# Delta rule and SoLU layer on one core: six batches of two chunks, off-diagonal Gram blocks copied by ScalarE from PSUM, first blocks of T read back by quarter

## Chip, cores and metric

The kernel runs on one core of one Trainium2 chip. The metric is device time in microseconds (us) for one execution. The median of three runs is 513.54 us (513.34 to 514.23). The core's engines run side by side, each in the order of its own program: PE (matmul), DVE, ACT, POOL, and SP, which here issues every DMA.

## What is computed

Two parts in a row. The first is a delta rule over 768 steps for 4 batches of 8 heads with 48 dimensions each; its output, seen as 3072 tokens of 384 numbers, goes through a layer with 1024 hidden units.

```python
k_n = k / (norm(k) + 1e-6)
for t in range(S):                       # S = 768
    y[t] = q[t] @ state
    v_old = k_n[t] @ state
    state = state + beta[t] * outer(k_n[t], v[t] - v_old)
x = y.transpose(0, 2, 1, 3).reshape(3072, 384)
h = x @ w_in                             # 384 x 1024
solu = h * softmax(h)
ln = (solu - mean) / sqrt(var + 1e-6) * g_ln
out = ln @ w_out                         # 1024 x 384
```

## The kernel before

**Tiling.** The 768 steps are cut into 12 chunks of C = 64. Within a chunk the recurrence is solved at once: with the Gram matrix of the chunk's keys a unit triangular 64x64 system has to be inverted for each (batch, head). The inverse is called T. Two batches with 8 heads each share the 128 partitions; such a pair is `bp`. A *unit* is one chunk of one pair, so there are 24 units, numbered here 0 to 23 (unit = 2 x chunk + pair). Each unit holds 128 tokens for the second part.

**Batches of inversions.** Inversion works on 32x32 diagonal blocks, one block for each partition ("lane"), for several units together. Such a group is a batch `m`; `chunks_of(m)` says which chunks it takes. Before, there are seven: chunk 0; chunks 1 and 2; 3 and 4; 5 and 6; 7 and 8; 9 and 10; chunk 11. So batches 0 and 6 have two units, the others four. For each batch:

- `load_kq`, `gram`: for each unit PE forms k k^T (`gram`) and k q^T (`qk`) in PSUM, ACT copies the first to `g`, DVE masks the second to `pm`, and SP stores `g` in DRAM as `gd`.
- `to_inv`: SP loads the diagonal blocks from `gd` into `ginv`, one block for each lane.
- `norms`: 19 small DVE operations on the diagonal (the first writes `rst`) give the norms of k, and two DVE products of 128x1024 prepare `ginv` and `y`. POOL then masks `y` (`affine_select`): this is the start of the inversion proper.
- `inv_step`: 30 steps, each a product `itmp` and a sum into `y`. In batches 0 and 1 DVE and POOL share them; in the others POOL does all.
- `inv_end`: ACT writes a transposed copy into `ginv`, SP stores `y` as `zd` and that copy as `xd`, and loads them back lane by lane: `zt` (diagonal blocks of T) and `gx`, `gy` (the off-diagonal Gram blocks from `gd`, the first diagonal blocks from `xd`).
- `tlevel`/`block_level`: for each unit two rounds of small matmuls (`mps<-zt,gx`, then `mps<-msb,gx` and `mps<-msb,gy`) give the off-diagonal block of T, which ACT copies into `zt`. They are called T1 and T2 below.

`chain(m, u)` then runs the recurrence for a unit: K·S (`kps`), the difference `r` on DVE, U = T r (`ups`), its state update (`cps`, into `st`) and the output `yps`, which is split into a high and a low half `xh`, `xl` and transposed by DMA (`xth`, `xtl`). `moe_h` forms h with 18 matmuls, its row maximum on DVE (the first `TENSOR_REDUCE st<-h` of a unit, used as its mark), exponent, product, sums and `pth`, `ptl`; `moe_out` has 24 matmuls `ops` with w_out, the correction by `csum` and the store `out_dram<-oc`.

**Order.** Nothing here is issued in the order in which it is written. A recorder collects all operations; `Recorder.order` is a list scheduler with its own costs, which picks for each engine the ready operation with the smallest priority, and `emit` (line 265) writes the result out. So every row of the profile has line L265, and tiles tell the operations apart. The priorities are numbers on a scale of units: chain of unit i at i, its h at i + 1.15, its output at i + 2.5. A batch whose first unit is f has its Gram products, its start (`begin`) and its T at fixed distances ahead of f; chain has an extra shift of -CH. On the chip each engine keeps the emitted order, and an instruction that waits holds up all that stand behind it on its engine. For SP this means that a DMA that waits for its data or its buffer holds up every later DMA.

Buffers come from small pools: `p10` is a ring of ten for the tags `kq` (kq tiles and the raw w_out), `ps_f` two PSUM buffers for `gram`, `qk` and `mps`, `ps_ch` two for the chain. Loads of w_in and w_out are converted by DVE, POOL and ACT (`wf`, `wg`, `wc_i`, `wc_o`) into two halves each; `column_sums` (`csum`) needs all of w_out.

Of the kernel before, what the change touches and what calls it, by code (L numbers as in the profile page):

```python
# [16 lines left out]
P = 128  # L17
C = 64
NC = S // C
NB = 7  # L20
CH = 1
SC = 64.0
SC2 = SC * SC
# [275 lines left out]


def chunks_of(m):
    return [ch for ch in (2 * m - 1, 2 * m) if 0 <= ch < NC]


@with_exitstack
def kernel(
# [223 lines left out]
    last0 = [None]  # L530

    def to_inv(m):
        gi = p2.tile([P, 32, 32], F32, tag="ginv", name=f"ginv_{m}")
        ginv[m] = gi
        for b in range(4):
            blk = b % 2
            for z in range(1 if len(units(m)) == 4 else 2):
                src = gdt[m].rearrange("t u h j -> t (u h) j")
                n = H * len(units(m))
                ls = slice(0, n)  # L540
                sp.dma_start(
                    kb=128, out=gi[32 * b + 16 * z : 32 * b + 16 * z + n],
                    in_=src[32 * b : 32 * b + 32, ls, blk * 32 : blk * 32 + 32].rearrange("j l i -> l j i"),
                )
# [32 lines left out]
    def inv_end(m):  # L577
        y, x1 = yt[m], ginv[m]
        act.copy(ns=1950, out=x1, in_=y.rearrange("p j i -> p i j"))
        zd = dr.tile([P, 32, 32], F32, tag="zd", name=f"zd_{m}")  # L580
        sp.dma_start(kb=512, out=zd, in_=y)
        xd = dr.tile([P, 32, 32], F32, tag="xd", name=f"xd_{m}")
        for r0 in (0, 64):
            sp.dma_start(kb=128, out=xd[r0 : r0 + 32], in_=x1[r0 : r0 + 32])
        zz = zt[m % 2]

        xx = p2.tile([P, 4 * H, 32], F32, tag="gx", name=f"gx_{m}")
        xy = p1.tile([P, 4 * H, 32], F32, tag="gy", name=f"gy_{m}")
        n = 16 * len(chunks_of(m))
        src = gdt[m].rearrange("t u h j -> t (u h) j")  # L590
        for b in range(4):
            blk = b % 2
            r0 = 32 * b
            rows = slice(r0, r0 + 32)
            sp.dma_start(kb=128, out=zz[rows, 0:n, blk * 32 : blk * 32 + 32], in_=zd[r0 : r0 + n].rearrange("l j i -> j l i"))
# [217 lines left out]
    for bp in range(2):
        add(once(-14 + .1 * bp, lambda bp=bp: load_kq(0, bp), lambda bp=bp: squares(bp)))
        add(gram(0, bp, -13.5 + .01 * bp))
        add(once(-9, lambda bp=bp: load_kv(0, bp), lambda bp=bp: fill_v(0, bp)))
        add(tlevel(0, bp, -12.9 + 0.1 * bp, -12.85 + 0.1 * bp))
# [12 lines left out]
    for m in range(1, NB):
        f = 4 * m - 2
        nu = len(units(m))
        e = f if m > 1 else f - 2.5
        for u in range(nu):
            tg = e - 9 + 0.9 * u if m > 1 else -11.2 + 0.05 * u
            ch, bp = units(m)[u]
            add(once(tg - 0.9 if m > 1 else -11.8, lambda ch=ch, bp=bp: load_kq(ch, bp)))
            add(gram(m, u, tg))  # L840
            t = e - 1.9 + 0.9 * u
# [5 lines left out]
        add(inversion(m, tn + 0.6, e - 2.6 if m > 1 else -10))  # L847
# [35 lines left out]
def _lay(q, k, v, beta, moe_w_in, moe_w_out, moe_g_ln):  # L883
# [45 lines left out]
```

## Time and profile before

| | |
|---|---|
| median of 3 runs | 513.54 us |
| profiled execution | 512.04 us |
| its span (first to last instruction) | 510.2 us |
| busy: PE, DVE, ACT, POOL | 368.2, 318.6, 192.9, 294.0 us |
| DMA | 180640 packets, 72.21 MB, queue 1 70.8% |
| granted TensorE clock, mean | 0.92 |

A row of the timeline gives the start (us from the span's start), the duration, the engine, the line, the operation, the tile written and those read, and the shapes; `xN` joins N equal ones in a row. In brackets stands how long the engine had been idle, and what ended that. SPq is SP's queue: there a row is the issue of a DMA, not its flight. In the groups of instructions the columns are busy time, mean duration in ns, and idle time before with its releaser. In the list of DMAs they are the count, the size of each and the median us from issue to landing.

### The profile page before, as it was taken

Reading aid. Unit: us, or ns where it says so; the run is one execution under the profiler, and the core shown is the slowest. Engines: PE = TensorE matmul, PEld = TensorE weight load, DVE = VectorE, ACT = ScalarE, POOL = GpSimd, SP = SyncE. Lnnn points to the kernel's source line nnn. Section 1 sums busy time; section 2 is a strip of 40 time slices with the busy share of each in tenths; the row PEclk is TensorE's granted clock in tenths of the full one; section 3 lists DMA queues with packets and bytes.
Section 4 is the critical chain, followed back from the end, with each engine's and each line's share of the span. In section 5 each row is a group of like instructions: output and inputs, shape, how many; then the busy total and the mean of one; then the engine's idle time right before and its main releaser. Section 6 shows DMA issues by size and latency. Waiting matters only on the chain.

```text
span 510.2 us, 18246 instructions
## 1 busy us (share of the span) xinstructions
PE 368.2 (72%) x7744; PEld 233.9 (46%) x7744; DVE 318.6 (62%) x791; ACT 192.9 (38%) x382; POOL 294.0 (58%) x506
## 2 busy tenths in 40 slices
PE   3510070689579488997598997787969797899974
PEld 3410070455346345665366564444635464566532
DVE  3599999887884383655088664256597355455670
ACT  2210241465522143536144544224345345454450
POOL 3378385966558998984016886008989898100000
PEclk9999999877876699998799998898989899999998
DMA  8685662987989949977999587985656866744332
GB/s 212 159 255 98 155 169 65 161 171 174 172 162 165 179 113 160 168 135 161 189 165 144 145 162 151 160 162 95 107 118 144 145 114 128 131 64 99 73 68 61
DMA packets 180640, 72.21 MB, mean 142 GB/s; under 512 B 165520, under 2 KB 168976, under 8 KB 180560
## 3 DMA queue, kind: packets, MB, share of 16 engines
q1 hardware_dynamic: 180560, 71.06, 70.8%
q8 instruction: 60, 0.98, 0.9%
q14 instruction: 20, 0.16, 0.1%
HBM read 37.21 MB, written 16.52 MB: 105 GB/s over the span
## 4 chain that ended last, share of the span: by engine, by line
POOL 28%; PE 22%; DVE 19%; issue 10%; DMA 9%; SPq 7%; ACT 4%; POOLq 0%; DVEq 0%; ACTq 0%
POOL y L265 13%; POOL itmp L265 11%; PE h L265 7%; SPq L265 7%; PE ops L265 7%; DVE y L265 5%; DVE itmp L265 4%; DMA zt<-zd 3%; DMA ginv<-gd 3%; PE mps L265 2%; DVE wf L265 2%; DVE rst L265 1%; DVE st L265 1%; PE kps L265 1%; PE yps L265 1%
## 5 line engine op out<-in xcount | busy, mean ns | idle before, releaser
L265 POOL TENSOR_TENSOR y<-y,itmp 128x84 f32<-128x84 f32 (+16 forms) x190 | 100.7, 530 | 14.6
L265 POOL TENSOR_TENSOR itmp<-y,ginv 128x84 f32<-128x84 f32 (+16 forms) x190 | 93.3, 491 | 14.0
L265 DVE TENSOR_REDUCE st<-h 128x1 f32<-128x1024 f32 x24 | 29.3, 1222 | 87.5 <-PE h L265 82.2
L265 PE MATMUL qk<-kq 48*64 48x64 f32 x768 | 40.4, 269 | 24.9 <-DVE pm L265 15.6
L265 PE MATMUL gram<-kq 48*64 48x64 f32 x768 | 43.2, 270 | 18.8 <-DMA kq<-kq_dram 11.5
L265 POOL TENSOR_TENSOR st<-st,nhalf 128x1 f32<-128x1 f32 x24 | 13.2, 551 | 64.1 <-DVE st L265 64.1
L265 PEld LDWEIGHTS gram<-kq 48*64 48x64 f32 x768 | 37.5, 178 | 25.7 <-ACT g L265 6.3
L265 PEld LDWEIGHTS <-pth 128*128 128x128 f16 x384 | 37.6, 99 | 25.5 <-issue 1.7
L265 PE MATMUL h<-win_hi,xtl 128*128 128x512 f16 x144 | 45.4, 419 | 5.3 <-DVE pr L265 2.6
L265 PE MATMUL mps<-zt,gx 32*32 32x32 f32 x768 | 13.5, 205 | 48.6 <-issue 28.9
L265 PE MATMUL h<-win_lo,xth 128*128 128x512 f16 x144 | 46.7, 421 | 1.7 <-POOL win_lo L265 1.7
L265 PEld LDWEIGHTS qk<-kq 48*64 48x64 f32 x768 | 35.8, 178 | 25.3 <-DVE pm L265 16.1
L265 PEld LDWEIGHTS <-xth 128*128 128x128 f16 x288 | 28.4, 105 | 39.7 <-issue 14.8
L265 PE MATMUL ops<-wout_hi,ptl 128*128 128x384 f16 x192 | 38.7, 345 | 8.7 <-DMA ptl<-pl 6.8
L265 PE MATMUL h<-win_hi,xth 128*128 128x512 f16 x144 | 43.4, 411 | 0.0
L265 ACT ACTIVATE e<-h,st 128x1024 f32<-128x1024 f32 x24 | 26.7, 1114 | 38.0 <-DVE st L265 26.4
L265 POOL TENSOR_SCALAR_AFFINE_SELECT y<-y 128x1024 f32<-128x1024 f32 x7 | 9.4, 1346 | 53.5 <-DVE y L265 53.5
L265 DVE TENSOR_SCALAR st<-st 128x1 f32<-128x1 f32 (+1 forms) x216 | 35.5, 165 | 5.6
L265 PE MATMUL ops<-wout_lo,pth 128*128 128x384 f16 x192 | 36.9, 334 | 0.0
L265 PEld LDWEIGHTS mps<-zt,gx 32*32 32x32 f32 x768 | 10.1, 117 | 56.9 <-issue 34.8
L265 PE MATMUL ops<-wout_hi,pth 128*128 128x384 f16 x192 | 35.5, 326 | 0.0
L265 PE MATMUL cps<-u,kv 64*64 64x48 f32 x704 | 28.9, 235 | 9.1 <-ACT u L265 3.2
(94 smaller groups left out, 860.4 us busy)
## 6 DMA issues: line engine op xcount, KB each, us to landing
kq<-kq_dram SPq DMA_DIRECT2D x48, 192.0 KB, 4.5
kv<-kv_dram SPq DMA_DIRECT2D x24, 384.0 KB, 4.3
gd<-g SPq DMA_DIRECT2D x48, 128.0 KB, 3.3
out_dram<-oc SPq DMA_DIRECT2D x24, 192.0 KB, 2.2
zd<-y SPq DMA_DIRECT2D x7, 512.0 KB, 2.6
wi<-w_in_dram SPq DMA_DIRECT2D x6, 512.0 KB, 4.4
wo<-w_out_dram SPq DMA_DIRECT2D x8, 384.0 KB, 4.0
ginv<-gd SPq DMA_DIRECT2D x20, 128.0 KB, 4.2
```

The source lines that it names most:

```text
L265: fn(*[real(a) for a in args], **{k: real(a) for k, a in kw.items()})
```

## The change

There are six batches of two whole chunks, four units each. Batch 0 now has four units (kn is loaded and squared for four; beta no longer has doubled entries). The off-diagonal Gram blocks no longer go through DRAM: ACT copies them from PSUM right after `g`, two copies of 32x256 for each unit, into `gx`. The first diagonal blocks of T were loaded twice, into `gx` and `gy`; now a tile `xx` takes each block once, in the partition quarter in which T2 reads it, with 16 DMAs of 16 KB for each batch. For batches 0 and 1 `zt` and `xx` are loaded in two halves, of two units each. The Gram products of batch 0 use the PSUM buffers of the chain, and two of its `g` copies the tile `e`. The raw w_in tiles share the ring `kq`, and their loads get an earlier priority. The priorities of `begin`, of batch 0's T and chain and of batch 2's Gram products are new numbers.

```diff
-NB = 7
+NB = NC // 2
 def chunks_of(m):
-    return [ch for ch in (2 * m - 1, 2 * m) if 0 <= ch < NC]
+    return [2 * m, 2 * m + 1]
...
     def load_w_in(k, q, t0, t1):
-        raw = p3.tile([P, 512], w_in.dtype, tag="pr", name=f"wi_{k}_{q}")
+        raw = (p3 if k < 2 and q < 1 or k < 1 else p10).tile([P, 512], w_in.dtype, tag="pr" if k < 2 and q < 1 or k < 1 else "kq", name=f"wi_{k}_{q}")
...
     def gram(m, u, t0):
         act.copy(out=g, in_=gps_)
+        if u == 0:
+            gxt[m] = p3.tile([P, 4 * H, 32], F32, tag="gx", name=f"gx_{m}")
+        for b2 in range(2):
+            act.copy(out=gxt[m][C * b2 + 32 : C * b2 + 64, H * u : H * u + H], in_=gps_[C * (1 - b2) + 32 : C * (1 - b2) + 64, :, 0:32])
...
     def inv_end(m):
-        xx = p2.tile([P, 4 * H, 32], F32, tag="gx", name=f"gx_{m}")
-        xy = p1.tile([P, 4 * H, 32], F32, tag="gy", name=f"gy_{m}")
...
-            if blk == 0:
-                for t, r1 in ((xx, r0), (xy, r0 + 32)):
-                    sp.dma_start(kb=128, out=t[r1 : r1 + 32, 0:n], in_=xd[r0 : r0 + n].rearrange("l j i -> j l i"))
-            else:
-                sp.dma_start(kb=128, out=xx[rows, 0:n], in_=src[rows, 0:n, 0:32])
+        xx = p2.tile([P, 4, 4, 32], F32, tag="xx", name=f"xx_{m}")
+        for us_ in ((0, 2), (2, 4)) if m < 2 else ((0, 4),):
+            n = us_[1] - us_[0]
+            l = slice(H * us_[0], H * us_[1])
+            for r0 in (0, 64):
+                lanes = slice(r0 + l.start, r0 + l.stop)
+                src = xd[lanes].rearrange("(u x h) j i -> j x u h i", u=n, x=2)
+                for u in range(n):
+                    for x in range(2):
+                        r1 = r0 + 32 * x
+                        sp.dma_start(kb=16, out=xx[r1 : r1 + 32, us_[0] + u], in_=src[:, x, u])
+                for blk in range(2):
...
+                    sp.dma_start(kb=32 * n, out=zz[rows, l, blk * 32 : blk * 32 + 32], in_=zd[lanes].rearrange("l j i -> j l i"))
...
-        f = 4 * m - 2
-        e = f if m > 1 else f - 2.5
+        f = 4 * m
...
-        tn = e - 5.4 if m > 1 else -10.8
+        tn = f - 5.4 if m > 2 else f - 7 if m > 1 else -10.8
...
-        add(chain(m, u, i, i + 0.13, i + 0.25), -CH)
+        add(chain(m, u, i, i + 0.13, i + 0.25), -CH if m else -14)
```

How this moves instructions is shown at three places. A name carries its batch, or its chunk and pair, and then a running number.

The first is DVE around its share of batch 1's inversion. Before, `itmp_1_30` is the last step of that inversion; then follow `wf` and `pm`, and only then the state `st_0` of the first chunk and its `xl_0_0`.

```order
L265 TENSOR_TENSOR itmp_1_30_0_1036<-y_1_657,ginv_1_553 128x10
L265 TENSOR_TENSOR y_1_657<-y_1_657,itmp_1_30_0_1036 128x10
L265 TENSOR_SCALAR wf_1_1_1041<-wi_1_1_479 128x512
L265 SCALAR_TENSOR_TENSOR wf_1_1_1041<-wi_1_1_479,wf_1_1_1041 128x512 x2
L265 TENSOR_TENSOR pm_3_0_1050<-qk_3_0_910,mask_93 128x512
L265 COPY st_0_1055<-cps_0_0_854 128x384
L265 SCALAR_TENSOR_TENSOR xl_0_0_1070<-yps_0_0_856,xh_0_0_921 128x384
```

After, the product that opens the inversion of batch 1 (`y_1`), then the state and `xl_1_0` of the second chunk, then the inversion's first step:

```order
L265 TENSOR_TENSOR y_1_1106<-ginv_1_874,nb_1_1072 128x1024
L265 TENSOR_SCALAR wg_0_1171<-wo_0_1079 128x384
L265 SCALAR_TENSOR_TENSOR wg_0_1171<-wo_0_1079,wg_0_1171 128x384
L265 TENSOR_TENSOR st_0_936<-st_0_936,cps_1_0_1134 128x384
L265 SCALAR_TENSOR_TENSOR xl_1_0_1202<-yps_1_0_949,xh_1_0_1193 128x384
L265 TENSOR_TENSOR itmp_1_1_0_1215<-y_1_1106,ginv_1_874 128x30
L265 TENSOR_TENSOR y_1_1106<-y_1_1106,itmp_1_1_0_1215 128x30
```

What moved: the chain of chunks 0 and 1 for pair 0 stood behind the whole inversion of batch 1 and now stands ahead of its first step.

The second is SP where the Gram blocks of batch 2 are loaded for the inversion (`ginv_2`), in the order after. `pth_0_1` and `ptl_0_1` belong to unit 1, `g_5_1` is the last Gram product of batch 2, and `xth_2_0` belongs to the chain of unit 4:

```order
L265 DMA kq_5_1_1952<-kq_dram 48x1024 x2
L265 DMA_TRANSPOSE pth_0_1_2000<-ph_0_1_1955 128x8x128
L265 DMA_TRANSPOSE ptl_0_1_2044<-pl_0_1_1996 128x8x128
L265 DMA kq_6_0_2062<-kq_dram 48x1024 x2
L265 DMA kq_6_1_2101<-kq_dram 48x1024 x2
L265 DMA gd_2_1390<-g_5_1_2105 64x512 x2
L265 DMA_TRANSPOSE xth_2_0_2156<-xh_2_0_2064 128x3x128
L265 DMA kq_7_0_2163<-kq_dram 48x1024 x2
L265 DMA ginv_2_2213<-gd_2_1390 32x32x32 x4
```

Before, `ginv_2` stood behind `gd_2<-g_4_1` and ahead of the transposes of unit 2's x; now it stands behind the loads of kq for chunk 6 and behind a transpose of unit 4. On PE that last Gram product now comes right after the state update `cps_2_0` of unit 4, the first unit of batch 1.

The third is SP between the inversions of batches 2 and 3. Before:

```order
L265 DMA ginv_3_2308<-gd_3_1837 32x32x32 x4
L265 DMA gd_4_2357<-g_7_0_2310 64x512 x2
L265 DMA gd_4_2357<-g_7_1_2360 64x512 x2
L265 DMA kv_4_0_2376<-kv_dram 128x768
L265 DMA gx_3_2399<-gd_3_1837 32x32x32 x2
L265 DMA_TRANSPOSE ptl_1_0_2434<-pl_1_0_2151 128x8x128
L265 DMA_TRANSPOSE pth_1_0_2459<-ph_1_0_2128 128x8x128
L265 DMA out_0_dram<-oc_0_0_2461 128x384
L265 DMA zd_2_2516<-y_2_1918 128x1024
L265 DMA xd_2_2557<-ginv_2_1770 32x1024 x2
```

After, from the last of the loads `zt_0<-zd_2` (the store `zd_2` itself stands seven rows above this piece; between them are `xd_2`, one store of an output, two other loads of `zt_0` and the 16 of `xx_2`):

```order
L265 DMA zt_0_217<-zd_2_2982 32x32x32 x2
L265 DMA_TRANSPOSE xth_3_1_3107<-xh_3_1_3070 128x3x128
L265 DMA_TRANSPOSE pth_2_1_3122<-ph_2_1_3093 128x8x128
L265 DMA_TRANSPOSE ptl_2_1_3150<-pl_2_1_3120 128x8x128
L265 DMA_TRANSPOSE xtl_3_1_3193<-xl_3_1_3102 128x3x128
L265 DMA ginv_3_3197<-gd_3_2363 32x32x32 x2
L265 DMA out_0_dram<-oc_2_0_3140 128x384
```

What moved: the loads `ginv_3` stood ahead of the store `zd_2`; now they stand behind it, behind the loads from it and behind four transposes. `ginv_4` and `ginv_5` stand in the same way behind `zd_3` and `zd_4`.

More of the change, by code (lines that the diff above doesn't have):

```diff
@@ L434 @@
     nrm, nnt, bb, gdt, pt = {}, {}, {}, {}, {}
-    kqt, kvt, ztx, gxt = {}, {}, {}, {}
+    kqt, kvt, ztx, gxt, xxt = {}, {}, {}, {}, {}
     def units(m):
@@ L441, in load_kq @@
         t = p10.tile([P, H, 2, C], F32, tag="kq", name=f"kq_{ch}_{bp}")
-        if ch > 4:
+        if ch > 5:
             rec.after = raws[-1]
@@ L464, in squares @@
         act.activation(sq, k, AF.Square)
-        for v in (u, u + 2):
-            dve.tensor_reduce(out=xs[0][:, v], in_=sq, op=ALU.add, axis=AX.X)
+        dve.tensor_reduce(out=xs[0][:, u], in_=sq, op=ALU.add, axis=AX.X)
     def norms(m):
@@ L501, in gram @@
         k = kqt[ch, bp]
-        g = p2.tile([P, H, C], F32, tag="g", name=f"g_{ch}_{bp}")
+        if m or u < 2:
+            g = p2.tile([P, H, C], F32, tag="g", name=f"g_{ch}_{bp}")
+        else:
+            if u == 2:
+                ge[0] = p1.tile([P, 2, H, C], F32, tag="e", name="g_0")
+            g = ge[0][:, u - 2]
         pm = p10.tile([P, H, C], F32, tag="pm", name=f"pm_{ch}_{bp}")
         pt[ch, bp] = pm
-        gps_ = ps_f.tile([P, H, C], F32, tag="fl", name=f"gram_{ch}_{bp}")
+        if m:
+            gps_ = ps_f.tile([P, H, C], F32, tag="fl", name=f"gram_{ch}_{bp}")
+        else:
+            gps_ = ps_ch.tile([P, H, C], F32, tag="ch", name=f"gram_{ch}_{bp}")
         pps = ps_f.tile([P, H, C], F32, tag="fl", name=f"qk_{ch}_{bp}")
@@ L529 @@
     ginv, yt = {}, {}
-    last0 = [None]
+    last0, ge = [None], [None]
     def to_inv(m):
@@ L534, in to_inv @@
         ginv[m] = gi
+        src = gdt[m].rearrange("t u h j -> t (u h) j")
         for b in range(4):
             blk = b % 2
[L537 to L544, printed above, removed]
+            r = slice(32 * b, 32 * b + 32)
+            sp.dma_start(kb=128, out=gi[r], in_=src[r, :, blk * 32 : blk * 32 + 32].rearrange("j l i -> l j i"))
     def inv_begin(m):
@@ L585, in inv_end @@
         zz = zt[m % 2]
-        xx = p2.tile([P, 4 * H, 32], F32, tag="gx", name=f"gx_{m}")
-        xy = p1.tile([P, 4 * H, 32], F32, tag="gy", name=f"gy_{m}")
[L589 to L595, printed above, removed]
-            if blk == 0:
-                for t, r1 in ((xx, r0), (xy, r0 + 32)):
-                    sp.dma_start(kb=128, out=t[r1 : r1 + 32, 0:n], in_=xd[r0 : r0 + n].rearrange("l j i -> j l i"))
-            else:
-                sp.dma_start(kb=128, out=xx[rows, 0:n], in_=src[rows, 0:n, 0:32])
-        ztx[m], gxt[m] = zz, (xx, xy)
+        xx = p2.tile([P, 4, 4, 32], F32, tag="xx", name=f"xx_{m}")
[10 more added lines that the diff above has]
+                for blk in range(2):
+                    rows = slice(r0 + 32 * blk, r0 + 32 * blk + 32)
+                    lanes = slice(rows.start + l.start, rows.start + l.stop)
+                    sp.dma_start(kb=32 * n, out=zz[rows, l, blk * 32 : blk * 32 + 32], in_=zd[lanes].rearrange("l j i -> j l i"))
+        ztx[m], xxt[m] = zz, xx
     def block_level(u, nm, zz, z0, groups, t0, t1):
@@ L640, in tlevel @@
         yield t0
-        gx, gy = gxt[m]
-        gx, gy = (x[:, H * u : H * u + H] for x in (gx, gy))
-        yield from block_level(u, f"{m}_{u}", ztx[m], H * u, [(range(4), gx, gx, 0), (range(4, 8), gx, gy, 32)], t0, t1)
+        gx, x = gxt[m][:, H * u : H * u + H], xxt[m][:, u]
+        yield from block_level(u, f"{m}_{u}", ztx[m], H * u, [(range(4), gx, x, 0), (range(4, 8), gx, x, 32)], t0, t1)
     st = {bp: cp.tile([P, H, D], F32, name=f"st_{bp}") for bp in range(2)}
@@ L812, in begin @@
         inv_begin(m)
[L815 to L819, printed above, removed]
+    for u, (ch, bp) in enumerate(units(0)):
+        add(once(-14 + .1 * u, lambda ch=ch, bp=bp: load_kq(ch, bp)))
+        add(once(-13.7 + .01 * u, lambda u=u: squares(u)))
+        add(gram(0, u, -13.5 + .01 * u))
+        add(once(-9 + u, lambda ch=ch, bp=bp: load_kv(ch, bp)))
+        add(once(-9 + u, lambda u=u: fill_v(0, u)))
+        add(tlevel(0, u, -5 + u, -4.95 + u), -8)
     add(once(-13.6, lambda: sp.dma_start(kb=112, out=bt, in_=beta)))
@@ L825 @@
     for i in range(6):
-        add(load_w_in(i // 2, i % 2, -11.5 if i < 2 else -11.0, -8 + 0.1 * i))
+        add(load_w_in(i // 2, i % 2, -13.3 + 0.01 * i, -8 + 0.1 * i))
     add(once(-8.5, load_g))
@@ L832 @@
     for m in range(1, NB):
-        f = 4 * m - 2
-        nu = len(units(m))
-        e = f if m > 1 else f - 2.5
-        for u in range(nu):
-            tg = e - 9 + 0.9 * u if m > 1 else -11.2 + 0.05 * u
-            ch, bp = units(m)[u]
+        f = 4 * m
+        for u, (ch, bp) in enumerate(units(m)):
+            tg = f - 9 + 0.9 * u if m > 1 else -11.2 + 0.05 * u
+            if m == 2:
+                tg = -2 + 0.9 * u
             add(once(tg - 0.9 if m > 1 else -11.8, lambda ch=ch, bp=bp: load_kq(ch, bp)))
             add(gram(m, u, tg))
-            t = e - 1.9 + 0.9 * u
+            t = f - 1.9 + 0.9 * u
             add(tlevel(m, u, t, t + 0.4))
@@ L844 @@
             add(once(f + u - 0.9, lambda m=m, u=u: fill_v(m, u)))
-        tn = e - 5.4 if m > 1 else -10.8
+        tn = f - 5.4 if m > 2 else f - 7 if m > 1 else -10.8
         add(begin(m, tn, tn + (0.5 if m > 1 else 0.01)))
-        add(inversion(m, tn + 0.6, e - 2.6 if m > 1 else -10))
+        add(inversion(m, tn + 0.6, f - 2.6 if m > 1 else -10))
     order = [(m, u) for m in range(NB) for u in range(len(units(m)))]
@@ L909, in _lay @@
     return {
-        "kn_dram": con(kn[0]),
+        "kn_dram": con(kn[:2].reshape(4, P, H, D)),
         "kv_dram": kv,
```

5 lines of the change are left out of this document (2 added, 3 removed).

## The prediction

> **What bounds the kernel now.** I read the page first: the shares of busy time, and the chain that ended last.
>
> ```profile
> span 510.2 us, 18246 instructions
> PE 368.2 (72%) x7744; PEld 233.9 (46%) x7744; DVE 318.6 (62%) x791; ACT 192.9 (38%) x382; POOL 294.0 (58%) x506
> ...
> POOL 28%; PE 22%; DVE 19%; issue 10%; DMA 9%; SPq 7%; ACT 4%; POOLq 0%; DVEq 0%; ACTq 0%
> POOL y L265 13%; POOL itmp L265 11%; PE h L265 7%; SPq L265 7%; PE ops L265 7%; DVE y L265 5%; DVE itmp L265 4%; DMA zt<-zd 3%; DMA ginv<-gd 3%; PE mps L265 2%; DVE wf L265 2%; DVE rst L265 1%; DVE st L265 1%; PE kps L265 1%; PE yps L265 1%
> ```
>
> No engine is full. The largest part of the chain is POOL's inversion (its products `itmp` and its sums `y`, 24% together). So I followed the inversions in the timeline. `TENSOR_SCALAR_AFFINE_SELECT y` on POOL opens one, the store `zd<-y` on SP closes it, and the first `mps<-zt,gx` on PE that waited for `zt<-zd` is the first use of its result.
>
> ```profile
> 230.46 0.35 SPq L265 DMA_DIRECT2D zd<-y  x1
> 250.75 0.64 PE L265 MATMUL mps<-zt,gx 32*32 32x32 f32 x30 [5.44 <-DMA zt<-zd]
> 270.88 1.26 POOL L265 TENSOR_SCALAR_AFFINE_SELECT y<-y 128x1024 f32<-128x1024 f32 x1 [4.95 <-DVE y L265]
> 310.96 0.36 SPq L265 DMA_DIRECT2D zd<-y  x1
> 324.67 0.45 PE L265 MATMUL mps<-zt,gx 32*32 32x32 f32 x30 [3.37 <-DMA zt<-zd]
> 344.46 1.26 POOL L265 TENSOR_SCALAR_AFFINE_SELECT y<-y 128x1024 f32<-128x1024 f32 x1 [29.61 <-DVE y L265]
> 385.77 0.34 SPq L265 DMA_DIRECT2D zd<-y  x1
> 400.00 0.45 PE L265 MATMUL mps<-zt,gx 32*32 32x32 f32 x30 [2.81 <-DMA zt<-zd]
> ```
>
> These are batches 3, 4 and 5. From batch 3's store to batch 4's are 80.5 us, to batch 5's another 74.8. Each such round has three steps: store to first use (20.3 us for batch 3, 13.7 for 4, 14.2 for 5), first use to the next select (20.1 and 19.8), and the inversion itself (40.1 and 41.3). Before its select of batch 5 POOL sat idle for 29.6 us, waiting for the DVE product that opens the inversion. The inversions are thus the resource that sets the pace, and half of each round they aren't running.
>
> It is not always so. Two rounds overlapped:
>
> ```profile
> 187.93 0.33 SPq L265 DMA_DIRECT2D zd<-y  x1
> 201.59 0.45 PE L265 MATMUL mps<-zt,gx 32*32 32x32 f32 x30 [1.92 <-DMA zt<-zd]
> ...
> 431.35 0.33 SPq L265 DMA_DIRECT2D zd<-y  x1
> 447.16 0.45 PE L265 MATMUL mps<-zt,gx 32*32 32x32 f32 x30 [2.40 <-DMA zt<-zd]
> 448.39 1.22 DVE L265 TENSOR_REDUCE st<-h 128x1 f32<-128x1024 f32 x1 [7.62 <-PE h L265]
> 460.56 1.23 DVE L265 TENSOR_REDUCE st<-h 128x1 f32<-128x1024 f32 x1 [4.49 <-PE h L265]
> 472.35 1.23 DVE L265 TENSOR_REDUCE st<-h 128x1 f32<-128x1024 f32 x1 [4.01 <-PE h L265]
> ```
>
> Batch 2 to 3 took 230.46 − 187.93 = 42.5 us and batch 5 to 6 took 431.35 − 385.77 = 45.6 us, because there SP issues the next batch's Gram loads before the store, not after it. Once nothing waits for an inversion, a unit (one chunk of one batch pair; its mark is the row maximum of h on DVE) takes 12 us: 448.39, 460.56, 472.35 are units 19, 20 and 21.
>
> **The change part by part.**
>
> *One inversion fewer.* Six batches of four units replace 2+4+4+4+4+4+2. A serial round of about 75 to 80 us goes, or an overlapped one of 43 to 46. But what counts is when the store comes that frees the last units. Before, the store of batch 5 (385.77) frees units 18 to 21 and the short batch 6 (431.35) only 22 and 23. After, the store of batch 5 is the last and frees 20 to 23.
>
> *Head.* The orders in the section on the change give this term.
>
> ```profile
> 52.97 0.34 SPq L265 DMA_DIRECT2D zd<-y  x1
> 60.09 1.72 POOL L265 TENSOR_SCALAR_AFFINE_SELECT y<-y 128x1024 f32<-128x1024 f32 x1 [8.30 <-DVE y L265]
> 63.32 0.64 PE L265 MATMUL mps<-zt,gx 32*32 32x32 f32 x30 [2.09 <-DMA zt<-zd]
> 76.43 1.30 SPq L265 DMA_TRANSPOSE xth<-xh  x1
> 87.91 0.35 SPq L265 DMA_DIRECT2D zd<-y  x1
> 90.28 0.37 PE L265 MATMUL qk<-kq 48*64 48x64 f32 x1 [14.61 <-DVE pm L265]
> ...
> 137.76 0.19 DVE L265 TENSOR_SCALAR rst<-ginv 128x32 int32<-128x32 int32 x1 [0.96 <-DMA ginv<-gd]
> 144.45 1.26 POOL L265 TENSOR_SCALAR_AFFINE_SELECT y<-y 128x1024 f32<-128x1024 f32 x1 [8.20 <-DVE y L265]
> ...
> 178.86 0.48 ACT L265 COPY csum<-cs 128x384 f32<-128x384 f32 x1 [6.45 <-PE cs L265]
> 185.50 1.23 DVE L265 TENSOR_REDUCE st<-h 128x1 f32<-128x1024 f32 x1 [0.68 <-ACT oc L265]
> ```
>
> Before, batch 1's inversion follows batch 0's at once (select 60.09, store 87.91), and the chain of chunk 0 waits behind it on DVE (PE idle 14.6 us up to 90.28). After, DVE has the chain's `st`, `r_1_0`, `st` and `xl_1_0` ahead of that inversion. With four units to load, I put batch 0's store at 56 (3 us later than 52.97) and its first use at 69.5, 13.5 behind, as for batch 4. From there to `xl_1_0`: 13 us to the transpose of x (76.43 − 63.32), its landing, 12 matmuls of h, two T levels, U and the state of the second chunk: 28 us, which I estimate from the steps before, so 98. Batch 1's inversion, split over DVE and POOL as batch 0's, takes 27.8 with its select (87.91 − 60.09): store at about 125, against 87.91.
>
> Batch 2 then waits for its last Gram product, which on PE stands behind the state of unit 4 and so behind batch 1's T. I take 12 us from store to first use, 19 for 22 matmuls of h, six T halves and unit 4's chain, and 11 for the Gram product, its copy, its store and its loads: 125 + 42 = 167 for the first op of the norms of batch 2 (137.76 before). Bounds: 150, if the second chunk needs only what the first did, and 182, if SP's loads of kq and w_out ahead of that load stall as well. To its store are 187.93 − 137.76 = 50.2 us: 217.
>
> What the head gets in return: `csum` can come earlier, since w_out's last conversions on POOL now stand before batch 2's inversion and not behind it; the stall of unit 3 (185.50) goes. But the inversions don't wait for it.
>
> *Three rounds, 2 to 5.* In the new order SP issues the Gram loads of batches 3, 4 and 5 all behind the store of the batch before, its 18 or more issues and some transposes. The overlaps of 42.5 and 45.6 are gone; all three rounds are serial. I take 15 + 20 + 41 = 76 each, from the rows of batches 4 and 5 with 1 us on the first step (next part): 228. Batch 5's store: 217 + 228 = 445.
>
> *Loads of the first blocks.* 16 issues of 16 KB replace the six of 128 KB (two each for `gx<-xd` and `gy<-xd`, two `gx<-gd`; the last two stood away from the store).
>
> ```profile
> 314.40 0.40 SPq L265 DMA_DIRECT2D zt<-zd  x1
> 314.97 0.56 SPq L265 DMA_DIRECT2D gx<-xd  x1
> 316.19 2.60 SPq L265 DMA_DIRECT2D zt<-zd  x2
> ...
> 320.36 0.86 SPq L265 DMA_DIRECT2D zt<-zd  x1
> ...
> zt<-zd SPq DMA_DIRECT2D x20, 128.0 KB, 4.2
> xd<-ginv SPq DMA_DIRECT2D x14, 128.0 KB, 2.0
> ```
>
> Batch 4's eight issues hold SP from 314.40 to 321.22, 6.8 us, with stalls such as 2.60 for two. Twenty issues at 0.40 are 8.0 us: +1.2, with less data behind them. No row shows a copy as small as 16 KB. Bounds: −1.5 us (the stalls go), and +6 (batch 3's 20.3 instead of 14.2); I take +1.
>
> The Trainium skill speaks against this part ("DMA: Bandwidth & Descriptors", Bandwidth): transfers under 64 KB are dominated by their descriptors, and its table gives 0.68 us at 4 KB and 0.95 us at 64 KB. If 16 such transfers ran one behind the other at some 0.75 us, an estimate from that page, they would take 12 us and each round would be 4 longer. Our rows have many copies in flight at once (2.0 us to land, 0.4 us apart), so I leave the sum as it is.
>
> *ScalarE's copies of the off-diagonal blocks.* Two for each unit, 48 in all.
>
> ```profile
> L265 ACT COPY zt<-mps 32x128 f32<-32x128 f32 x96 | 24.3, 254 | 10.8 <-PE mps L265 9.3
> L265 ACT COPY g<-gram 128x512 f32<-128x512 f32 x24 | 14.0, 583 | 36.3 <-PE qk L265 23.9 <-DMA kq<-kq_dram 6.8 <-PE gram L265 3.2
> ```
>
> 254 ns at 128 elements and 583 at 512 give 0.36 us at 256, so 17.5 us on an engine that is 38% busy. They hold the PSUM buffer 0.73 us longer and delay the ACT work queued behind. Bounds: 0, and 17.5 if all of it came onto the path. I take 0: a round has 41 us of inversion in which ACT isn't awaited.
>
> *Traffic.* Fewer packets, by about 4,000 for each of six batches and a whole batch besides; DMA appears in the chain with 9%, and the path pays latency there, not volume. I take nothing, up to a few us gained.
>
> *Tail.* From T of batch 6 (447.16) to the end of the span are 63.0 us, with four marks still to come in full and unit 19's at 448.39. In the new order T of batch 5 stands within unit 18's h and before unit 17's output product, one unit earlier: 63 + 14 (a unit of 12 and the chains of unit 20) = 77. First use is at 445 + 15 = 460, the end at 537.
>
> **Sum.** 217 + 228 + 15 + 77 = 537 us of span, against 510.2. The profiled execution took 512.04, so 1.84 us lie outside the span: 538.9. That execution was 1.5 us below the median of 513.54; the forecast, rounded, is 539.
>
> **Rivals.** *Faster.* The head slips less or the rounds are shorter. The deciding point: the end is first norms op of batch 2 + 50.2 + 228 + 92, so with 76 a round it breaks even at 140, nearly the 137.76 of before. At 150 for the head and 68 a round (13.7 + 14 + 40.5, if the next batch's products stand ready as soon as the loads are issued) the span is 150 + 50 + 204 + 88 = 492, the time 494. For it: unit 3's stall goes, and one batch with its whole round goes. Against it: the two orders above, and POOL's wait of 29.6 us, which is a wait for work that stands behind T.
>
> *Slower by the queue.* If 16 issues behave as batch 3's did, each of four uses comes 5 to 6 us later: 539 + 22 = 561. For it: the stalls of 2.6 us in SP. Against: the packets are fewer. The page's price above gives about 555.
>
> *Slower by ScalarE.* If the 17.5 us came onto the path, 539 + 17 = 556. Against: ACT has 4% of the chain.
>
> *The same.* Head and rounds happen to cancel within 1 us; nothing in the profile makes it likely.
>
> **Chances.** Forecast 0.55, slower by the queue 0.13, by ScalarE 0.07, faster 0.22, same 0.03. Within 0.2% is about what a measurement of this kernel can tell from no change. The range 505 to 560 takes the head's bounds (150 gives 522, 182 gives 554), the copies' bounds and half of the faster case.
>
> **What would show it.** Right: a store of batch 1 near 125, norms of batch 2 near 167, stores 2 to 5 some 76 us apart, POOL idle for about 30 us before the selects of batches 3 to 5, a first use 15 us after each store. Wrong: batch 2's norms before 145, two stores less than 60 us apart, or a tail from batch 5's first use well under 70. `xx` landing long after `zt`, or idle PE until an ACT copy of `gx`, would speak for the other two.

## The result, and the profile after

| | before | after |
|---|---|---|
| median | 513.44 us (4 runs) | 558.34 us (4 runs, 555.43 to 560.84) |
| ratio after to before | | 1.0875, 95% interval 1.0813 to 1.0937 |
| profiled execution, span | 512.04, 510.2 us | 557.12, 555.3 us |
| granted TensorE clock, mean | 0.92 | 0.868 |
| DMA packets, share of queue 1 | 180640, 70.8% | 152753, 58.1% |

The change makes the kernel 44.9 us slower; the forecast was 539, 25.6 us slower, with a range of 505 to 560. Two of the four executions of run e11 below fell into a slower state of the chip (515.98 and 517.47 us) and are left out of its figures. The profile's page after, its first lines and the chain that ended last:

```profile
span 555.3 us, 18238 instructions
PE 385.0 (69%) x7744; PEld 247.1 (45%) x7744; DVE 305.1 (55%) x771; ACT 209.9 (38%) x430; POOL 257.4 (46%) x445
...
POOL 27%; PE 18%; issue 11%; DVE 11%; SPq 10%; DMA 8%; ACT 3%; POOLq 0%; DVEq 0%; ACTq 0%
```

POOL works 36.6 us less (one inversion fewer), and DMA moves some 28,000 packets fewer. Yet every engine but ACT has a smaller share of a longer span: the time went into waits. SP's queue has grown from 7% to 10% of the chain that ended last.

The timeline, with the rows that answer to those of before: first operation of the norms (`rst<-ginv`), select, store and first use. The bracket of a select tells how long POOL sat idle before it.

```profile
128.41 0.33 SPq L265 DMA_DIRECT2D zd<-y  x1
...
177.03 0.48 ACT L265 COPY csum<-cs 128x384 f32<-128x384 f32 x1 [1.73 <-PE cs L265]
181.55 0.19 DVE L265 TENSOR_SCALAR rst<-ginv 128x32 int32<-128x32 int32 x1 [5.74 <-DMA ginv<-gd]
...
227.30 0.35 SPq L265 DMA_DIRECT2D zd<-y  x1
245.07 0.64 PE L265 MATMUL mps<-zt,gx 32*32 32x32 f32 x30 [5.13 <-DMA zt<-zd]
261.05 1.26 POOL L265 TENSOR_SCALAR_AFFINE_SELECT y<-y 128x1024 f32<-128x1024 f32 x1 [30.65 <-DVE y L265]
301.01 0.34 SPq L265 DMA_DIRECT2D zd<-y  x1
...
380.46 0.35 SPq L265 DMA_DIRECT2D zd<-y  x1
...
458.20 0.32 SPq L265 DMA_DIRECT2D zd<-y  x1
476.77 0.64 PE L265 MATMUL mps<-zt,gx 32*32 32x32 f32 x30 [4.92 <-DMA zt<-zd]
```

These are the stores of batches 1 to 5. The three rounds from batch 2 to 5 take 73.7, 79.5 and 77.7 us: all serial, the overlaps are gone. From batch 5's first use to the end are 555.3 − 476.77 = 78.5 us. Before batch 3's select POOL waits 30.65 us, before batch 4's 34.67 and before batch 5's 15.34 (there a small operation on `kv` at 401.13 lies in between).

What happens in the first part of a round is seen in SP's queue, from the loads behind the store of batch 2 (at 227.30) to the Gram loads of batch 3:

```profile
230.63 0.39 SPq L265 DMA_DIRECT2D zt<-zd  x1
231.26 4.86 SPq L265 DMA_DIRECT2D xx<-xd  x8
236.16 0.43 SPq L265 DMA_DIRECT2D zt<-zd  x1
236.64 4.71 SPq L265 DMA_DIRECT2D xx<-xd  x8
241.40 1.04 SPq L265 DMA_DIRECT2D zt<-zd  x2
242.53 1.19 SPq L265 DMA_TRANSPOSE xth<-xh  x1
...
246.48 1.25 SPq L265 DMA_TRANSPOSE xtl<-xl  x1
247.79 1.18 SPq L265 DMA_DIRECT2D ginv<-gd  x2
...
249.62 2.10 SPq L265 DMA_DIRECT2D ginv<-gd  x2
```

SP issues almost without a gap from 230.63 to 251.72. A 16 KB copy holds it here for 4.86 / 8 = 0.61 us, no less than a `zt` of 128 KB (0.39 and 0.43). Over all 96 copies of `xx` the mean is 0.50 us; the sixteen of a batch take 9.6, 8.7, 8.5 and 8.4 us for batches 2 to 5. They stand ahead of the last `zt`, which T needs, and ahead of `ginv`, which the next inversion needs.

### The profile page after: what moved, and what is told of

Read it like the earlier page. It is cut to its first block, busy times and chain, and to the rows that moved or that the text cites. A ratio compares the mean times of both kernels' runs of the same rounds, so it can differ in the third digit from the quotient of the medians.

```text
span 555.3 us, 18238 instructions
## 1 busy us (share of the span) xinstructions
PE 385.0 (69%) x7744; PEld 247.1 (45%) x7744; DVE 305.1 (55%) x771; ACT 209.9 (38%) x430; POOL 257.4 (46%) x445
## 2 busy tenths in 40 slices
DMA packets 152753, 68.14 MB, mean 123 GB/s; under 512 B 137568, under 2 KB 141280, under 8 KB 152672
## 3 DMA queue, kind: packets, MB, share of 16 engines
q1 hardware_dynamic: 152672, 66.98, 58.1%
## 4 chain that ended last, share of the span: by engine, by line
POOL 27%; PE 18%; issue 11%; DVE 11%; SPq 10%; DMA 8%; ACT 3%; POOLq 0%; DVEq 0%; ACTq 0%
POOL y L265 13%; POOL itmp L265 12%; SPq L265 10%; PE h L265 7%; PE ops L265 5%; DVE y L265 3%; DMA zt<-zd 2%; DVE itmp L265 2%; PE ups L265 2%; PE mps L265 2%; POOL st L265 1%; DMA xd<-ginv 1%; PE kps L265 1%; DVE st L265 1%; DMA ptl<-pl 1%
## 5 line engine op out<-in xcount | busy, mean ns | idle before, releaser
L265 POOL TENSOR_TENSOR y<-y,itmp 128x84 f32<-128x84 f32 (+16 forms) x160 | 80.1, 501 | 12.5
L265 POOL TENSOR_TENSOR itmp<-y,ginv 128x84 f32<-128x84 f32 (+16 forms) x160 | 76.9, 481 | 11.8
L265 POOL TENSOR_SCALAR_AFFINE_SELECT y<-y 128x1024 f32<-128x1024 f32 x6 | 8.0, 1339 | 108.8 <-DVE y L265 58.8
L265 PE MATMUL h<-win_hi,xtl 128*128 128x512 f16 x144 | 45.3, 422 | 11.6 <-DMA xtl<-xl 7.9
L265 PE MATMUL ops<-wout_hi,ptl 128*128 128x384 f16 x192 | 41.2, 364 | 12.0 <-DMA ptl<-pl 7.2
L265 POOL TENSOR_TENSOR st<-st,nhalf 128x1 f32<-128x1 f32 x24 | 13.2, 551 | 70.0 <-DVE st L265 69.9
L265 PEld LDWEIGHTS <-xth 128*128 128x128 f16 x288 | 28.6, 105 | 36.6 <-issue 10.9
L265 DVE SCALAR_TENSOR_TENSOR pl<-pr,st,ph 128x1024 f16<-128x1024 f32 x24 | 32.3, 1344 | 19.4 <-ACT ph L265 18.8
L265 PE MATMUL h<-win_hi,xth 128*128 128x512 f16 x144 | 41.9, 401 | 0.0
L265 PE MATMUL yps<-st,kq 48*64 48x48 f32 x704 | 32.3, 253 | 9.3 <-DVE xl L265 9.2
L265 PE MATMUL ops<-wout_lo,pth 128*128 128x384 f16 x192 | 38.4, 344 | 0.0
L265 PE MATMUL ops<-wout_hi,pth 128*128 128x384 f16 x192 | 38.0, 341 | 0.0
```

What stands on the lines that cost most here:

```text
L265: fn(*[real(a) for a in args], **{k: real(a) for k, a in kw.items()})
```

## The experiments

All are compared with the kernel before, run on the same chip (medians 514.64, 515.33, 515.32 and 514.96 us in the four groups e1 to e4, e5 to e8, e9 to e11, e12). For the changed kernel the ratio to hold against is 1.0875.

**e1: batch 1 early.** The head, first by its first link. The two lines hold for batch 0 as well as for batch 1.

```diff
-  tg = f - 9 + 0.9 * u if m > 1 else -11.2 + 0.05 * u
+  tg = f - 9 + 0.9 * u if m > 1 else -13.34 + 0.005 * u
-  add(once(tg - 0.9 if m > 1 else -11.8, lambda ch=ch, bp=bp: load_kq(ch, bp)))
+  add(once(tg - 0.9 if m > 1 else -13.38, lambda ch=ch, bp=bp: load_kq(ch, bp)))
```

> Priorities of batch 1's kq loads and Gram products put ahead of batch 0's inversion; its inversion then stands right behind batch 0's on DVE and POOL and ahead of the chain of chunk 0. Theory (the head's loss starts with batch 1's late inversion): store of batch 1 near 95 instead of 128.4, first norms operation of batch 2 at 150 to 160 instead of 181.6, all later stores earlier by the same 20 to 30, total 530 to 540. Rival (batch 2's start is held by what stands between, the conversions of w_out, the ring of kq and the Gram product behind unit 4's chain, whatever batch 1 does): store of batch 1 near 95 but norms of batch 2 later than 175, total within 1% of 558.

Measured: 563.04 us, ratio 1.0958 (1.0898 to 1.1018). Timeline of e1, the store of batch 1 and the first norms operation of batch 2:

```profile
112.66 0.33 SPq L265 DMA_DIRECT2D zd<-y  x1
...
184.84 0.19 DVE L265 TENSOR_SCALAR rst<-ginv 128x32 int32<-128x32 int32 x1 [1.77 <-DMA ginv<-gd]
```

Batch 1's store came 15.8 us earlier (33 were expected), and batch 2 started 3.3 us later than in the changed kernel. The theory that the head's loss is handed on from batch 1 falls; the rival holds, apart from the size of the first step.

**e6: batch 2's kq early.** The other link of the head: the ring of ten that kq shares with the raw tiles of w_out.

```diff
-  add(once(tg - 0.9 if m > 1 else -11.8, lambda ch=ch, bp=bp: load_kq(ch, bp)))
+  add(once(-3 if m == 2 else tg - 0.9 if m > 1 else -11.8, lambda ch=ch, bp=bp: load_kq(ch, bp)))
```

> The changed kernel with the kq loads of batch 2 (chunks 4 and 5) put ahead of the loads of w_out in the ring that they share; the last Gram product of batch 2 then no longer waits for a buffer that w_out's raw tiles hold. Theory (that ring and SP's queue set the start of batch 2): first norms operation of batch 2 at 160 to 172 instead of 181.6, and the total falls by 8 to 20 us. Rival (the head doesn't pass its time on: the next round is gated by the units' own work): norms earlier, but the store of batch 3 less than 5 us earlier and the total within 1% of 558.

Measured: 554.53 us, ratio 1.0801 (1.0744 to 1.0858). Timeline of e6, norms of batch 2, then the stores of batches 2, 3 and 5:

```profile
165.14 0.18 DVE L265 TENSOR_SCALAR rst<-ginv 128x32 int32<-128x32 int32 x1
...
215.98 0.34 SPq L265 DMA_DIRECT2D zd<-y  x1
...
295.06 0.36 SPq L265 DMA_DIRECT2D zd<-y  x1
...
452.36 0.32 SPq L265 DMA_DIRECT2D zd<-y  x1
```

That was the link: the norms of batch 2 come 16.4 us earlier (165.14 for 181.55). The edit changes one priority; the scheduler then moved other rows as well, on every engine. But the store of batch 2 is only 11.3 earlier, that of batch 3 6.0, that of batch 5 5.8, and the ratio falls by 0.0074, less than the intervals tell apart. Both answers hold in part: the place of these loads set the start of batch 2, and a third of what is won there reaches batch 5's store. Whether the ring or the place in SP's queue holds them wasn't told apart.

**e2: inversions started earlier.** The rounds.

```diff
-  if m == 2:
-      tg = -2 + 0.9 * u
+  if m >= 2:
+      tg = f - 10 + 0.9 * u
-  tn = f - 5.4 if m > 2 else f - 7 if m > 1 else -10.8
+  tn = f - 7 if m > 1 else -10.8
```

> Start of the inversions of batches 3 to 5 and their Gram products put to the distances that batch 2 has (7 and 10 units ahead instead of 5.4 and 9). SP then issues the Gram loads of batch 3 ahead of the store of batch 2; those of batches 4 and 5 still stand behind the stores, but nearer. Theory (the rounds are serial because of the place of those loads): store 2 to store 3 takes 42 to 50 us instead of 73.7, the other two 65 to 75 instead of 79.5 and 77.7, total 510 to 530. Rival (the first use of T gates the next batch's norms in any case, or PE is full): rounds stay above 70, total above 545.

Measured: 538.79 us, ratio 1.0499 (1.0452 to 1.0546). Timeline of e2, Gram loads and norms of batch 3, store of batch 2, select of batch 3, store of batch 3:

```profile
214.20 3.12 SPq L265 DMA_DIRECT2D ginv<-gd  x4
...
220.70 0.40 DVE L265 TENSOR_SCALAR rst<-ginv 128x32 int32<-128x32 int32 x1 [3.12 <-DMA ginv<-gd]
...
227.28 0.35 SPq L265 DMA_DIRECT2D zd<-y  x1
...
232.30 1.27 POOL L265 TENSOR_SCALAR_AFFINE_SELECT y<-y 128x1024 f32<-128x1024 f32 x1
...
274.20 0.52 SPq L265 DMA_DIRECT2D zd<-y  x1
```

The Gram loads and norms of batch 3 now run ahead of the store of batch 2, POOL goes on without a wait, and the round takes 46.9 us instead of 73.7. In the next two the loads (from 285.37 and 360.37) still stand behind the stores (274.20 and 345.81), and they take 71.6 and 75.5. So the place of these loads makes the rounds serial; the Gram products and loads of kq, which the edit moves too, come earlier in all three rounds. The store of batch 5 lies at 421.27 instead of 458.20, 36.9 earlier, but the end only 21.8 earlier (span 533.5). From batch 5's first use to the end are now 92.9 us instead of 78.5: with the inversions ahead, the units' own work is late next.

**e3: four large copies of `xx`.** The order on PE, DVE, ACT and POOL is the same, row for row; SP has 4 issues where it had 16.

```diff
-  xx = p2.tile([P, 4, 4, 32], F32, tag="xx", name=f"xx_{m}")
+  xx = p1.tile([P, 4 * H, 32], F32, tag="xx", name=f"xx_{m}")
...
-  for u in range(n):
-      for x in range(2):
-          r1 = r0 + 32 * x
-          sp.dma_start(kb=16, out=xx[r1 : r1 + 32, us_[0] + u], in_=src[:, x, u])
+  for x in range(2):
+      r1 = r0 + 32 * x
+      sp.dma_start(kb=16 * n, out=xx[r1 : r1 + 32, l], in_=xd[lanes].rearrange("l j i -> j l i"))
```

> xx is loaded by 4 copies of all 32 lanes (128 KB each; both quarters get every block, so twice the bytes) instead of 16 copies of 16 KB; two halves of 64 KB for batches 0 and 1. The order on the other engines is the same. Theory (the sixteen issues cost SP some 0.5 us each and lie between a store and the first use): store to first use of batches 2 to 5 falls from 17.8, 16.9, 16.8, 18.6 to 13 to 15, total falls by 10 to 20 us. Rival (bytes and packets count, not issues): store to first use stays or grows by 1 to 3 us, total within 1% of 558 or above.

Measured: 537.79 us, ratio 1.0458 (1.0398 to 1.0518). SP's queue of e3 behind the store of batch 3, and below it the list of DMAs (KB of one, us to landing), first of the changed kernel, then of e3:

```profile
290.36 0.34 SPq L265 DMA_DIRECT2D zd<-y  x1
...
293.93 0.40 SPq L265 DMA_DIRECT2D zt<-zd  x1
294.43 1.25 SPq L265 DMA_DIRECT2D xx<-xd  x2
295.73 2.31 SPq L265 DMA_DIRECT2D zt<-zd  x1
298.08 1.30 SPq L265 DMA_DIRECT2D xx<-xd  x2
299.43 1.44 SPq L265 DMA_DIRECT2D zt<-zd  x2
```

```profile
xx<-xd SPq DMA_DIRECT2D x96, 16.0 KB, 1.9
```

```profile
xx<-xd SPq DMA_DIRECT2D x16, 128.0 KB, 4.1
```

The loads take SP 6.9 us (293.93 to 300.87) instead of 11.0 for the same batch in the changed kernel (304.58 to 315.54; 11.8 for batch 2, in the queue above), although they move twice the bytes of `xx`; the longer landing (4.1 us for 1.9) is covered: the first uses lie 13.4, 13.6, 13.6 and 16.5 us behind the stores of batches 2 to 5. The gain is 18.3 us of span, by term: 6.9 at the norms of batch 2 (174.66), 11.6 in the three rounds (69.9, 74.6, 74.8), and nothing net behind batch 5's store. The theory holds. Besides, SP is held 48.4 us by all copies of `xx` in the changed kernel and 21.4 us in e3.

**e4 and e12: ScalarE's copies twice.** Both kernels issue each copy a second time, e4 in the changed kernel, e12 in the one of e5 below.

```diff
+  for o in done:
+      t = o.calls[0][2].get("out")
+      if o.eng == "ACT" and isinstance(t, View) and t.root.name.startswith("gx_"):
+          o.calls = o.calls * 2
   with tc.manual_schedule():
```

> Each of the 48 ScalarE copies of an off-diagonal Gram block is issued twice in a row (17.8 us more of ScalarE at 0.37 us each); same order everywhere. Theory (these copies lie beside the inversions and cost nothing): within 0.5%, at most 3 us slower. Rival (they hold PSUM buffers and the work behind them on ScalarE): 8 to 18 us slower, above all in the head where Gram products wait for buffers.

> The seven-batch kernel with the new copies (521.8 us, 6.5 above the kernel before on its chip), each ScalarE copy of an off-diagonal block issued twice in a row, same order. Theory (the 6.5 us come from the changed order, the copies are covered): 518 to 526. Rival (the 6.5 us are the price of the copies): 526 to 531, and more where they delay U.

Measured: e4 560.96 us, ratio 1.0899 (1.0847 to 1.0952), against 1.0875. e12 522.33 us, ratio 1.0138 (1.0076 to 1.0200), against e5's 1.0138. The groups of ScalarE in the changed kernel, and in e4:

```profile
L265 ACT COPY gx<-gram 32x256 f32<-32x256 f32 x48 | 17.5, 364 | 0.8
```

```profile
L265 ACT COPY gx<-gram 32x256 f32<-32x256 f32 x96 | 35.0, 365 | 2.4
```

The copies take just what was interpolated (364 ns), and 17.5 us more of them move neither kernel by more than its runs scatter (the intervals are some 3 us to each side). They are covered.

**e5 and e9: seven batches with the new copies.** e5 gives the kernel before ScalarE's copies and a tile `xx` that is loaded whole (two copies of 128 KB for each pair of lanes); batches and priorities stay. e9 is e5 with `xx` by quarter, and SP aside its order is e5's, row for row.

```diff
 e5:
...
+  for b2 in range(2):
+      act.copy(out=gxt[m][C * b2 + 32 : C * b2 + 64, H * u : H * u + H], in_=gps_[C * (1 - b2) + 32 : C * (1 - b2) + 64, :, 0:32])
...
-  for t, r1 in ((xx, r0), (xy, r0 + 32)):
-      sp.dma_start(kb=128, out=t[r1 : r1 + 32, 0:n], in_=xd[r0 : r0 + n].rearrange("l j i -> j l i"))
-  else:
-      sp.dma_start(kb=128, out=xx[rows, 0:n], in_=src[rows, 0:n, 0:32])
+  for r1 in (r0, r0 + 32):
+      sp.dma_start(kb=128, out=xx[r1 : r1 + 32, 0:n], in_=xd[r0 : r0 + n].rearrange("l j i -> j l i"))
 e9, against e5:
+  for x, r1 in enumerate((r0, r0 + 32)):
+      for l0 in range(4 * x, n, H):
+          sp.dma_start(kb=1024 / n, out=xx[r1 : r1 + 32, l0 : l0 + 4], in_=xd[r0 + l0 : r0 + l0 + 4].rearrange("l j i -> j l i"))
```

> The kernel before (seven batches, its priorities) with the new source of the blocks alone: ScalarE copies the off-diagonal Gram blocks from PSUM, the loads of these from DRAM go, and the first blocks of T are loaded whole into each quarter (2 copies of 128 KB for each pair of lanes, as before). Theory (the copies on ScalarE cost nothing; the loss is the six-batch order and the sixteen issues): within 1% of the kernel before. Rival (the ScalarE copies cost their 17.5 us in the head and at the Gram products): 523 to 532 us.

> The seven-batch kernel with the new copies (521.8 us), its first blocks of T now loaded by quarter, 16 copies of 16 KB for a batch of four units and 8 for one of two, half the bytes; same order on every other engine. Theory (each small issue costs SP 0.5 us between a store and its first use, in any kernel whose rounds are serial): 12 issues more in place of 4 give 4 to 6 us for each of the serial rounds 3, 4, 5 and the last use, less in the overlapped ones: 535 to 548. Rival (the cost belongs to the six-batch order): 517 to 527.

Measured: e5 521.80 us, ratio 1.0138 (1.0078 to 1.0198); e9 541.01 us, ratio 1.0483 (1.0434 to 1.0533). Timeline of e9, store and first use of batch 4, 20.1 us apart (16.5 in e5):

```profile
328.28 0.36 SPq L265 DMA_DIRECT2D zd<-y  x1
...
348.34 0.64 PE L265 MATMUL mps<-zt,gx 32*32 32x32 f32 x30 [8.36 <-DMA zt<-zd]
```

The sixteen small copies cost seven batches 19.2 us, as they cost six 20.5 (558.34 − 537.79, e3): the price belongs to them, not to the order of six. e5 missed its expectation by a little, 0.4% above the 1%. By e12 the copies on ScalarE aren't the reason; a changed order is a likely one, which isn't shown.

**e7, e8, e10, e11: the losses taken out together.** e7 joins e2 and e3. e8 adds e6, with w_out's conversion one unit earlier and inversions starting 7.5 units ahead. e10 and e11 use other numbers in the same table. The edits of e10 against the changed kernel, beside those of e3:

```diff
-  add(load_w_in(i // 2, i % 2, -13.3 + 0.01 * i, -8 + 0.1 * i))
+  add(load_w_in(i // 2, i % 2, -11.5 + 0.01 * i, -8 + 0.1 * i))
...
-  add(load_w_out(i, -1 + 0.05 * i, 2.1 + 0.05 * i))
+  add(load_w_out(i, -1 + 0.05 * i, 1.1 + 0.05 * i))
...
+  if m > 2:
+      tg = f - 10 + 0.6 * u
...
-  add(once(tg - 0.9 if m > 1 else -11.8, lambda ch=ch, bp=bp: load_kq(ch, bp)))
+  add(once(-2.5 + .05 * u if m == 2 else tg - 0.9 if m > 1 else -11.8, lambda ch=ch, bp=bp: load_kq(ch, bp)))
...
-  t = f - 1.9 + 0.9 * u
+  t = f - 2.2 + 0.9 * u
...
-  tn = f - 5.4 if m > 2 else f - 7 if m > 1 else -10.8
+  tn = f - 7.5 if m > 2 else f - 7 if m > 1 else -10.8
```

> The earlier starts of the inversions and the four large copies of xx together. If the two losses are independent (19.5 and 20.5 us from the medians of the two runs), total 515 to 522; if they share one cause (both shorten the way from a store to the next inversion), 525 to 535.

> All three: kq of batch 2 early, starts of the inversions still earlier (7.5 and 10 units ahead, Gram products closer together), w_out's conversion one unit earlier, xx in four large copies. If the head passes on its time, 500 to 512, below the kernel before; if not, 515 to 525.

> Six batches, xx in four large copies, other numbers in the table of priorities: kq of batch 2 early, inversions start 7.5 units ahead, Gram products closer together, T 0.3 units earlier, w_in later, w_out's conversion one unit earlier. Theory (with both losses gone, six batches save what the seventh round cost): 498 to 511, below the kernel before. Rival (the units' own work and the head are the bound now, and no place of the inversions helps): 512 to 520.

> As the run before it, and the Gram products and the inversion of batch 1 right behind batch 0's, w_out loaded earlier. Theory: 498 to 511. Rival (as e1 showed, the earlier batch 1 isn't passed on): 512 to 525.

| run | median us | ratio to before | 95% interval |
|---|---|---|---|
| e7 | 515.74 | 1.0008 | 0.9980 to 1.0036 |
| e8 | 514.88 | 0.9989 | 0.9957 to 1.0020 |
| e10 | 502.22 | 0.9751 | 0.9704 to 0.9798 |
| e11 | 508.77 | 0.9871 | 0.9826 to 0.9915 |

In e7 the two losses prove independent: ratio 1.0875 falls to 1.0008, slightly more than e2 and e3 take out one by one (1.0875 − 1.0499 and 1.0875 − 1.0458, together 0.0793). Six batches then run as long as seven did. e8 (514.88) lies at the lower edge of its second answer: the head's time wasn't passed on here either. e10 is faster than both kernels; its timeline, the store of batch 5 and its first use:

```profile
385.81 0.33 SPq L265 DMA_DIRECT2D zd<-y  x1
...
406.52 0.45 PE L265 MATMUL mps<-zt,gx 32*32 32x32 f32 x30 [2.05 <-DMA zt<-zd]
```

The last store comes 72.4 us earlier than in the changed kernel, the end 54.8 earlier (span 500.5). From the store to the end are now 114.7 us instead of 97.1: so it is no longer the inversions that set the end, but more likely the units' own work. Which of e10's numbers does how much wasn't taken apart. e11, with batch 1's inversion early as in e1, gains less than e10; other numbers of the two differ as well, so this isn't put down to one of them.

## Why the prediction was right, and where it was off

**Serial rounds.** Right, and the largest part. The forecast was 3 x 76 = 228; the rows give 230.9. e2 shows the reason given to be the cause: with the Gram loads ahead of the store the round of 73.7 becomes 46.9, while the two with the loads behind it stay above 70. That the sum came out so near is partly luck: without the sixteen issues (e3) the three rounds take 219.3, where the forecast without its 1 us a round has 225.

**One inversion fewer.** Right: POOL works 36.6 us less and gains nothing by it, since the last four units wait for batch 5's store, at 458.20.

**The tail.** 77 forecast, 78.5 measured.

**The head.** Mis-sized by 14.5 us: batch 2's norms at 167, measured 181.55, at the edge of the bounds given (150 to 182). Batch 1's store was forecast well (125, measured 128.41). The terms behind it, "125 + 42", were each too small: 12.9 us to the first use (12 forecast), 22.7 from there to the Gram product (19), 17.5 from it to the norms (11). The way itself is in the trace of the changed kernel: on PE the Gram product (it opens with the row `qk`) follows unit 4's state update (`cps`) at once. Its kq, though, had come only just before.

```profile
156.48 0.51 SPq L265 DMA_DIRECT2D wo<-w_out_dram  x1
157.10 1.69 SPq L265 DMA_DIRECT2D kq<-kq_dram  x2
...
162.31 0.31 PE L265 MATMUL cps<-u,kv 64*64 64x48 f32 x1 [6.21 <-ACT u L265]
...
164.02 0.33 PE L265 MATMUL qk<-kq 48*64 48x64 f32 x1
```

The step that failed is taking that way for the only one. The kq of chunk 5, which belongs to batch 2 only since the batches are whole, stands on SP behind the loads of w_out, with which it shares the ring of ten buffers; it landed at 163.20. e1 moved batch 1's store by 15.8 us and unit 4's state update to 156.85, but kq landed at 162.29 and batch 2 didn't follow. e6 gave only the loads of kq another priority; the Gram product came at 137.72, ahead of unit 4's chain, and batch 2's norms 16.4 us earlier. The forecast had named these loads, but only as its upper bound (182). From the norms to batch 2's store it was 45.8 us instead of 50.2, which gave 4.4 back.

Batch 1 itself stood late for a second reason that the forecast didn't have. Its norms, in the timeline of the changed kernel:

```profile
92.11 0.19 DVE L265 TENSOR_SCALAR rst<-ginv 128x32 int32<-128x32 int32 x1 [10.71 <-DMA ginv<-gd]
```

DVE waited 10.71 us for the Gram loads before the chain on DVE came into play: the select of batch 1 came at 99.14, `xl_1_0` only at 102.60. How much each of the two holds wasn't singled out, so the good fit of 125 is partly luck.

**The sum over the head.** The forecast added the head to all that follows. e6 and e8 show that this holds to a third: 16.4 us at the start of batch 2 become 5.8 at batch 5's store. By the rows the miss of 18.3 us in the span (537 forecast, 555.3 measured) is made up of 10.3 at batch 2's store, 2.9 in the rounds, 3.6 at batch 5's first use and 1.5 in the tail. By e6 the error of 14.5 us at the start explains less of it than these rows suggest, and 558.34 lies only 1.7 us inside the upper end of the range.

**`csum`.** Hardly as told: it was to come earlier, and came at 177.03 for 178.86; the stall of unit 3 stays (its mark at 199.72).

**Loads of the first blocks.** Mis-sized. I took 0.40 us for each of twenty issues, 8.0 us in place of 6.8, and +1 us for each round, with +6 as the bound. Measured are 10.8 to 11.8 us for the twenty (batches 2 to 4); first uses lay 17.8, 16.9, 16.8 and 18.6 us behind the stores, against 15. And the price wasn't counted in full: the issues stand ahead of `ginv` too, and there are as many in the head. All of it was 20.5 us (e3), 19.2 in seven batches (e9). That is the rival "slower by the queue", with its price (22) nearly met and a chance of 0.13, which was too little. It too came about otherwise than told: the first uses came 2.6 to 4.4 us later than the 14.2 of before, not 5 to 6, and a good third of the gain of e3 (6.9 of 18.3) lies in the head. Without the sixteen issues the change cost 23 (537.79 against 514.64), where the forecast had 25.6 with 1 us a round for them.

The Trainium skill's rule that was weighed there ("DMA: Bandwidth & Descriptors", Bandwidth: transfers under 64 KB are dominated by their descriptors) told the right side, and the 555 worked out from its price is nearer than 539. The mechanism of that estimate, transfers one behind the other, isn't what the trace shows: the copies take 1.9 us to land and overlap, and what adds up is their issues on SP, 0.50 us each on average.

**ScalarE's copies.** Right at zero (e4, e12), and 364 ns for the 0.36 interpolated.

**Traffic.** Right at nothing: 15% fewer packets, and the kernel is slower. e3 moves more bytes than the changed kernel and is faster.

## What to carry to other kernels

When a change splits a load into many small ones, count what an issue costs on its queue, and all that stands behind it there, not the bytes: sixteen copies of 16 KB for a batch in place of four of 128 KB cost this kernel 20 us in all, with half the data. A resource that is busy half the time is bound by the way back to its next start; look in the instruction order for the load that starts it, and try it ahead of the wait. A time won at the start is worth at the end only what no other limit takes back on the way, so a sum of terms needs a second look at each joint.

## What the runs showed of the hardware

The time that SP takes for an issue falls little with the size. Its median is 0.43 us for the 96 copies of `xx` of 16 KB in the changed kernel (mean 0.50), and 0.49 for the 32 of 64 and 128 KB in e3 (mean 0.67, with waits up to 2.4):

```profile
L265 SPq DMA_DIRECT2D xx<-xd x96: 303/430/1390, 65.3 to 472.7; - x96
```

```profile
L265 SPq DMA_DIRECT2D xx<-xd x32: 303/488/2411, 66.0 to 450.9; - x32
```

The three numbers are the least, the median and the longest duration in ns.

The changed kernel was granted a lower mean TensorE clock (0.868 for 0.92). Within one kernel a difference of 0.04 hardly shows in the time: executions of e9 at 0.873 and 0.912 took 540.43 and 542.27 us, and of the kernel before at 0.89 and 0.927 took 514.06 and 514.76. No run gives the changed kernel itself the higher clock, so a few of the 44.9 us aren't excluded.
